# Spreading a maximum by a repeated stationary operand, one aggregate for the rest tile's statistics, and y's bound and the S sums placed earlier

## The chip, the core and the metric

One core of one Trainium2 chip. The time is device microseconds of one execution; times of several runs of a kernel are compared by their median. In the trace PE is TensorE (PEld its weight loads), DVE is VectorE, ACT is ScalarE, POOL is GpSimd and SP is SyncE, which issues most transfers.

## What is computed

Eight batches of 576 tokens go through three stages: attention by 32 memory slots per head (8 heads of 64), a channel and token mixer with width 512 and hidden width 2048, and a gated unit with a spatial product over the tokens.

```python
a = softmax(phi, axis=2)                       # over the tokens
k_m, v_m = a.T @ k, a.T @ v                    # 32 memory slots a head
x = softmax(q @ k_m.T / 8) @ v_m               # heads side by side: 576 x 512
u = x + (x.T @ U @ V).T
x = u + relu(u @ w_ch1) @ w_ch2
h = relu(x @ w_in); u, v = h[:, :512], h[:, 512:]
v = (v - mean(v)) / sqrt(var(v) + 1e-6)        # over the 512 channels
out = (u * (w_spatial @ v + b[:, None])) @ w_out
```

## The kernel before

The tokens of a batch stand in two halves of 288 columns (`TH`) or in five tiles of 128 rows, the last with 64 (the rest tile, `s == 4`). Most products run in fp16 with each operand split into a high and a low part, three matmuls for one (`HI`). Before a split the operand is scaled by a power of two found from its largest magnitude. That magnitude lies in one column, a value for each of 128 partitions, and must be known in all of them: `bmax_a` (L149) masks the exponent and scales a bf16 identity by it, which gives a diagonal; `bmax_b` (L157) multiplies the diagonal by ones, so that each partition holds all 128 values, and reduces them. GpSimd then clamps the result.

Batch 0 runs in fp32 while the weights are converted and split, with a filler that hands out that work between matmuls. Batch 1 runs the plain fp16 form (`w1_phase`, `w2_phase`, each for the halves `th` 0 and 1) and makes the sums S1 to S4 of blocks of w2 (`s_prep`, generator `sq`: load a quarter of w2, four additions, four splits, store; 11 steps a quarter, 44 in all), which batches 2 to 7 use in `st_phase`, a product with fewer multiplications. Each batch ends with its v and u tiles in the order of `V_ORDER` (`n` normalises a v tile, `y` scales the second half of y, `y_finish`), the spatial product (`spatial`) and the output product (`out_half`).

The attention of the next batch is a generator (`att`, L549). It does a step at each `yield`, and the phases call `step(nxt)` between their matmuls: in batch 1 through `w2_phase`'s `fill` (32 calls a half) and `both`, in later batches at 8 places of the first loop of `st_phase`, at each second of the first 18 of its 28 later places in the first half, and at two of three of the places of `late` in the second half, once `y_finish(b, 0)` is through; then one step behind each v or u tile. What is left is drained before the spatial phase. A "W" from it stops steps that are not asked for with `w` set.

The order on each engine is made at compile time by a scheduler that takes instructions in the order of the code where they are ready; inside `manual_schedule` (the first part of `st_phase`, and `first`) the code's order is kept as it is. PSUM holds five buffers `mm` and three buffers `at`.

In `att`, `mx` is the softmax maximum over the tokens for each memory slot, in a column a group; `dgx` holds two scaled identities, and `ones32` spreads them (L563). `scores(i)` is the i-th group of q times k_m, `ahl` the attention weights in two parts, the loop at L682 their product with U (`pps`), and `apr_sum` the result's windows. `behind_ghl` ties the reduction of phi to a place behind the spatial phase's first half.

In `v_tile` the rest tile holds its 64 rows twice, 256 channels in each half of the partitions, so that the two halves' means and variances are combined by hand (L1124 to L1136). `v_rsqrt` takes an inverse root in 13 small steps, and `v_norm` of tiles 2 to 4 waits for it.

Of the kernel before, what the change touches and what calls it, by code (L numbers as in the profile page):

```python
# [30 lines left out]
def mixer_kernel(  # L31
# [117 lines left out]
    def bmax_a(am, n=128):  # L149
        e = tiny(1, I32)  # L150
        dve.tensor_single_scalar(e[:n], am[:n].bitcast(I32), EXP_MASK, op=ALU.bitwise_and)
        dg = tp.tile([128, 128], BF16, tag="dgb", name="dgb", bufs=3)
        dve.tensor_scalar(out=dg[:n, :n], in0=identb[:n, :n], scalar1=e[:n].bitcast(F32),
                          scalar2=None, op0=ALU.mult)
        return dg

    def bmax_b(dg, o, n=128):  # L157
        ps = mm_tile()
        pe.matmul(ps[:, :n], onesb[:n, :], dg[:n, :n], start=True, stop=True)
        t = tiny()  # L160
        dve.tensor_reduce(out=t, in_=ps[:, :n], axis=AX.X, op=ALU.max)
        ps2(pool, o, t, 2.0 ** -60, ALU.max, 2.0 ** 60, ALU.min)

# [71 lines left out]
    def scale_w(name, am, n):  # L235
        dg = bmax_a(norm_bound(am, n))
# [3 lines left out]
        bmax_b(dg, C("m" + name))  # L240
# [58 lines left out]
    def first(vr):  # L299
# [7 lines left out]
        def spread(dg, n=128):  # L307
            ps = mm_tile()
            pe.matmul(ps[:, :n], onesb[:n, :], dg[:n, :n], start=True, stop=True)
            return ps  # L310

        def found(ps, o, n=128):
            t = tiny()
            dve.tensor_reduce(out=t, in_=ps[:, :n], axis=AX.X, op=ALU.max)
            ps2(pool, o, t, 2.0 ** -60, ALU.max, 2.0 ** 60, ALU.min)

# [17 lines left out]
        dgx = t1k()  # L334
        for g in range(2):
            dve.tensor_scalar(out=dgx[:, g * 128:(g + 1) * 128], in0=ident, scalar1=sc[:, g:g + 1],
                              scalar2=None, op0=ALU.mult)
        mxb = at_tile()
        pe.matmul(mxb[:, 0:256], ones32, dgx, start=True, stop=True)
# [39 lines left out]
        bu = bmax_a(norm_bound(amu, 1))  # L379
# [17 lines left out]
        bv = bmax_a(norm_bound(amv[:96], 2), 96)  # L397
# [151 lines left out]
    def att(b):  # L549
# [3 lines left out]
        dgx = t1k()  # L553
        with ExitStack() as es:
# [3 lines left out]
            for g in range(2):  # L558
                dve.tensor_scalar(out=dgx[:, g * 128:(g + 1) * 128], in0=ident, scalar1=sc[:, g:g + 1],
                                  scalar2=None, op0=ALU.mult)  # L560
# [81 lines left out]
        for gi, grp in enumerate(G):  # L642
# [28 lines left out]
            if gi == 0 and b > 2:  # L671
                scores(1)
                scores(2)
# [1074 lines left out]
```

## Time and profile before

| | us |
|---|---|
| median of 3 runs | 1134.02 (1133.17 to 1134.29) |
| profiled execution | 1134.62, span 1132.8 |

| engine | busy us | share | instructions |
|---|---|---|---|
| PE | 1112.1 | 98% | 12362 |
| PEld | 868.4 | 77% | 12365 |
| DVE | 842.9 | 74% | 2217 |
| ACT | 619.6 | 55% | 1350 |
| POOL | 89.5 | 8% | 316 |

The page's chain of work that ended last is 77% TensorE, 12% VectorE, 5% ScalarE and 2% transfers. A busy time is the union of the instructions' spans, and matmuls overlap in them: the distance from one start to the next is what a matmul costs the stream, its own duration is longer. In a timeline, neighbours of one kind are merged into one line, with the count behind an x, and a bracket gives the idle time of the engine before the line and what ended it.

### The profile page before, as it was taken

Reading aid. Unit: us, or ns where it says so; the run is one execution under the profiler, and the core shown is the slowest. Engines: PE = TensorE matmul, PEld = TensorE weight load, DVE = VectorE, ACT = ScalarE, POOL = GpSimd, SP = SyncE. Lnnn points to the kernel's source line nnn. Section 1 sums busy time; section 2 is a strip of 40 time slices with the busy share of each in tenths; the row PEclk is TensorE's granted clock in tenths of the full one; section 3 lists DMA queues with packets and bytes.
Section 4 is the critical chain, followed back from the end, with each engine's and each line's share of the span. In section 5 each row is a group of like instructions: output and inputs, shape, how many; then the busy total and the mean of one; then the engine's idle time right before and its main releaser. Section 6 shows DMA issues by size and latency. Waiting matters only on the chain.

```text
span 1132.8 us, 29695 instructions
## 1 busy us (share of the span) xinstructions
PE 1112.1 (98%) x12362; PEld 868.4 (77%) x12365; DVE 842.9 (74%) x2217; ACT 619.6 (55%) x1350; POOL 89.5 (8%) x316
## 2 busy tenths in 40 slices
PE   8899999999999999999999999999999999999998
PEld 6466767767677896788867887778967888679966
DVE  6767688878876786867776787867868687766764
ACT  4768765746546455564465454564555543653543
POOL 2101011000110001100010000100011000200000
PEclk9999999999999999999999999999999999999999
DMA  9879841351526230442316303262305303120201
GB/s 350 314 270 331 282 173 59 117 148 38 176 92 217 80 123 28 167 141 70 128 62 233 96 22 137 103 207 70 128 22 185 106 12 128 49 106 2 114 15 43
DMA packets 54855, 145.74 MB, mean 129 GB/s; under 512 B 7808, under 2 KB 37248, under 8 KB 43584
## 3 DMA queue, kind: packets, MB, share of 16 engines
q1 hardware_dynamic: 54208, 143.16, 35.9%
q8 instruction: 97, 1.59, 0.6%
q10 hardware_dynamic: 512, 0.67, 0.2%
q14 instruction: 38, 0.31, 0.1%
HBM read 120.32 MB, written 23.49 MB: 127 GB/s over the span
## 4 chain that ended last, share of the span: by engine, by line
PE 77%; DVE 12%; ACT 5%; DMA 2%; issue 2%; POOL 1%; SPq 0%; ACTq 0%; DVEq 0%; POOLq 0%
PE mm L923 17%; PE mm L957 13%; PE mm L1222 10%; PE mm L1252 8%; PE mm L1181 6%; PE mm L1110 6%; PE mm L818 4%; PE at L759 2%; PE at L578 2%; PE mm L795 1%; PE mm L841 1%; DMA gw<-in_kv_dram 1%; PE mm L878 1%; DMA wsr<-w2d 1%; DVE tmp L655 1%
## 5 line engine op out<-in xcount | busy, mean ns | idle before, releaser
L923 PE MATMUL mm<-gw,w2r 128*128 128x144 f16 x2304 | 169.6, 226 | 0.0
L923 PEld LDWEIGHTS <-w2r 128*128 128x128 f16 x2304 | 152.7, 98 | 8.7 <-issue 4.0
L957 PE MATMUL mm<-apr,z 128*128 128x288 f16 x1152 | 155.1, 286 | 0.0
L957 PEld LDWEIGHTS <-z 128*128 128x128 f16 x1152 | 109.7, 98 | 28.2 <-issue 2.0
L923 PE MATMUL mm<-gw,wa 128*128 128x144 f16 x1728 | 129.7, 226 | 0.0
L961 ACT ACTIVATE wsr<-mm 128x288 f32<-128x288 f32 x192 | 78.1, 407 | 92.5 <-PE mm L957 48.2
L1222 PE MATMUL mm<-wsr,gw 128*128 128x288 f16 x896 | 114.5, 286 | 1.7 <-ACT gw L1185 1.6
L923 PEld LDWEIGHTS <-wa 128*128 128x128 f16 x1728 | 111.1, 98 | 4.5 <-issue 1.0
L1222 PEld LDWEIGHTS <-gw 128*128 128x128 f16 x896 | 85.6, 98 | 32.2 <-issue 9.6
L1181 PE MATMUL mm<-yhl,gw 128*128 128x288 f16 x768 | 99.0, 286 | 0.0
L1252 PE MATMUL mm<-ghl,wa 128*128 128x288 f16 x768 | 97.8, 286 | 0.0
L1252 PEld LDWEIGHTS <-wa 128*128 128x128 f16 x768 | 74.4, 98 | 22.8 <-issue 3.8
L1181 PEld LDWEIGHTS <-gw 128*128 128x128 f16 x768 | 73.5, 98 | 19.0 <-issue 0.9
L1110 PE MATMUL mm<-gw,yhl 128*128 128x512 f16 x384 | 85.8, 379 | 1.3 <-ACT yhl L1076 1.3
L963 DVE TENSOR_TENSOR wsr<-wsr 128x288 f32<-128x288 f32 x96 | 44.0, 458 | 58.0 <-ACT wsr L961 58.0
L945 DVE TENSOR_TENSOR gw<-wsr,gw 128x720 f16<-128x720 f32 x96 | 85.5, 900 | 0.0
L1237 ACT ACTIVATE ghl<-gw,ysc 128x288 f16<-128x288 f32 x64 | 34.2, 535 | 83.0 <-DVE gw L1236 83.0
L944 ACT ACTIVATE gw<-wsr 128x720 f16<-128x720 f32 x96 | 76.4, 796 | 0.5
L1110 PEld LDWEIGHTS <-yhl 128*128 128x128 f16 x384 | 36.7, 98 | 43.6 <-ACT yhl L1076 1.6
L818 PE MATMUL mm<-gw,w2r 128*128 128x288 f32 x256 | 66.4, 409 | 0.1
L1116 DVE BATCH_NORM_STATS2 tiny<-tmp 128x6 f32<-128x512 f32 (+1 forms) x40 | 25.6, 639 | 46.0 <-ACT tmp L1114 46.0
L818 PEld LDWEIGHTS mm<-gw,w2r 128*128 128x128 f32 x256 | 47.4, 190 | 15.0 <-issue 1.9
(312 smaller groups left out, 1855.0 us busy)
## 6 DMA issues: line engine op xcount, KB each, us to landing
wa<-w1d SPq DMA_DIRECT2D x22, 1024.0 KB, 5.1
kvt<-in_kv_dram SPq DMA_DIRECT2D x28, 516.0 KB, 5.3
gw<-wid SPq DMA_DIRECT2D x12, 1024.0 KB, 7.8
wsr<-wsd SPq DMA_DIRECT2D x7, 1440.0 KB, 6.1
out_dram<-tmp SPq DMA_DIRECT2D x64, 144.0 KB, 1.9
gw<-in_w_dram SPq DMA_DIRECT2D x6, 1024.0 KB, 9.1
wa<-wod SPq DMA_DIRECT2D x6, 1024.0 KB, 4.8
qt<-in_qT_dram SPq DMA_DIRECT2D x23, 256.0 KB, 3.5
```

Of the source, the lines that this page charges most:

```text
L818: pe.matmul(ps, w2r[:, f, d * 128:(d + 1) * 128], AT[0]["g"][:, f, :], start=False, stop=(f == 15))
L923: pe.matmul(ps[:, dd * QH:(dd + 1) * QH], w(c, dd, 1 - x), gs[:, m, c, y, :], start=(first and c == 0 and dd == 0 and i == 0), stop=(end a ...
L944: act.activation(h, X[:, 3:8], func=ACTF.Copy)
L945: dve.tensor_tensor(out=gs[:, 2:7, c, 1, :], in0=X[:, 3:8], in1=h, op=ALU.subtract)
L957: pe.matmul(ps, a["z"][:, k, x, f * 128:(f + 1) * 128], a["apr"][:, k, y, sl], start=(i == 0), stop=(i == 5))
L961: act.activation(o, pair(ps), func=ACTF.Relu, scale=CG)
L963: dve.tensor_tensor(out=X[:, 4:6], in0=X[:, 2:4], in1=X[:, 1:3], op=ALU.subtract)
L1110: pe.matmul(ps, yhl[:, k, x, s * 128:(s + 1) * 128], wih[:, k, 0, 1 - y, :], start=(i == 0), stop=(i == 11))
L1181: pe.matmul(ps, wih[:, k, 1, 1 - x, d * 128:(d + 1) * 128], a["yhl"][:, k, y, sl], start=(i == 0), stop=(i == 11))
L1222: pe.matmul(pss[d], vn[:, s, x if s < 4 else 0, ds], wsh[:, s, th, 1 - y, :], start=(s == 0 and i == 0), stop=(s == 4 and i == 1))
L1237: act.activation(ghl[:, d, 0, sl], u2, func=ACTF.Identity, scale=sgt)
L1252: pe.matmul(ps, (wo0 if b else woh)[:, k, 1 - x, d * 128:(d + 1) * 128], a["ghl"][:, k, y, sl], start=(i == 0), stop=(i == 11))
```

## The change

- `bmax_a` and `bmax_b` go. `spread` makes the maximum itself the stationary operand, the upper 16 bits of each fp32 value repeated over 128 columns, and moves the bf16 identity through it; `found` reduces, masks the exponent and clamps; `bmax` is both. Every caller passes the column in place of the diagonal.
- The softmax maximum is spread by a transpose of its repeated column, one for each group, without `dgx`.
- In `att` from batch 3 on, `scores(2)` moves one step later; the product with U yields after slice 1 and after slice 3, in place of after slice 2, which makes one step more.
- `y_scale` is the first part of `y_finish`. For the second half it is called right behind v tile 0.
- The rest tile copies its raw statistics across the halves and aggregates once.
- In batch 1 the attention steps at three of four places of `w2_phase(b, 0)`, `sq` already steps at every second place of `w1_phase(b, 1)`, `both` has new numbers, and the rest of `sq` with the loads behind it moves from the end of `w2_phase(b, 1)` to behind v tile 0 and `y_scale`.

```diff
@@ -146,20 +146,20 @@
-    def bmax_a(am, n=128):
-        e = tiny(1, I32)
-        dve.tensor_single_scalar(e[:n], am[:n].bitcast(I32), EXP_MASK, op=ALU.bitwise_and)
-        dg = tp.tile([128, 128], BF16, tag="dgb", name="dgb", bufs=3)
-        dve.tensor_scalar(out=dg[:n, :n], in0=identb[:n, :n], scalar1=e[:n].bitcast(F32),
-                          scalar2=None, op0=ALU.mult)
-        return dg
-
-    def bmax_b(dg, o, n=128):
+    def spread(am, n=128):
         ps = mm_tile()
-        pe.matmul(ps[:, :n], onesb[:n, :], dg[:n, :n], start=True, stop=True)
+        pe.matmul(ps[:, :n], am[:n].bitcast(BF16)[:, 1:2].to_broadcast([n, 128]), identb[:n, :n],
+                  start=True, stop=True)
+        return ps
+
+    def found(ps, o, n=128):
         t = tiny()
         dve.tensor_reduce(out=t, in_=ps[:, :n], axis=AX.X, op=ALU.max)
+        dve.tensor_single_scalar(t.bitcast(I32), t.bitcast(I32), EXP_MASK, op=ALU.bitwise_and)
         ps2(pool, o, t, 2.0 ** -60, ALU.max, 2.0 ** 60, ALU.min)
+
+    def bmax(am, o):
+        found(spread(am), o)
@@ -331,12 +321,9 @@
         dve.tensor_reduce(out=sc[:, 0:2], in_=mt[:, 0:256].rearrange("p (g c) -> p g c", g=2), axis=AX.X, op=ALU.max)
-        dgx = t1k()
+        mxb = at_tile()
         for g in range(2):
-            dve.tensor_scalar(out=dgx[:, g * 128:(g + 1) * 128], in0=ident, scalar1=sc[:, g:g + 1],
-                              scalar2=None, op0=ALU.mult)
-        mxb = at_tile()
-        pe.matmul(mxb[:, 0:256], ones32, dgx, start=True, stop=True)
+            pe.transpose(mxb[:, g * 128:(g + 1) * 128], sc[:, g:g + 1].to_broadcast([128, 128]), ident)
         warm(14, mm_tile)
@@ -550,17 +537,14 @@
         mx = sc[:, 0:2]
-        dgx = t1k()
         with ExitStack() as es:
 ...
             dve.tensor_reduce(out=mx, in_=a["phiT"], axis=AX.X, op=ALU.max)
-            for g in range(2):
-                dve.tensor_scalar(out=dgx[:, g * 128:(g + 1) * 128], in0=ident, scalar1=sc[:, g:g + 1],
-                                  scalar2=None, op0=ALU.mult)
         yield
         mxb = at_tile()
-        pe.matmul(mxb[:, 0:256], ones32, dgx, start=True, stop=True)
+        for g in range(2):
+            pe.transpose(mxb[:, g * 128:(g + 1) * 128], sc[:, g:g + 1].to_broadcast([128, 128]), ident)
         e = a["e"]
@@ -670,9 +653,10 @@
                 scores(1)
+            yield
+            if gi == 0 and b > 2:
                 scores(2)
-            yield
-            if gi < 2 and b < 3:
+            elif gi < 2 and b < 3:
                 scores(gi + 1)
@@ -683,7 +667,9 @@
                           start=(s == 0 and y == 0), stop=(s == NST - 1 and y == 1))
-            if s == 2:
+            if s == 1:
+                yield
+            if s == 3:
                 yield
@@ -896,7 +881,7 @@
         dve.tensor_reduce(out=t, in_=am, axis=AX.X, op=ALU.max)
-        return y32, bmax_a(t)
+        return y32, t
@@ -1060,14 +1045,21 @@
-    def y_finish(b, th, y32, dg):
+    def y_scale(b, th, ym):
+        ysc = AT[b]["ysc"]
+        o = th * 8
+        my, ry, cs = (ysc[:, o + i:o + i + 1] for i in range(3))
+        bmax(ym, my)
+        recip(ry, my)
+        ps2(pool, cs, ry, 2.0 ** 13, ALU.mult)
+
+    def y_finish(b, th, y32, ym):
         a = AT[b]
 ...
         my, ry, cs, s_in, inv = (ysc[:, o + i:o + i + 1] for i in range(5))
-        bmax_b(dg, my)
-        recip(ry, my)
-        ps2(pool, cs, ry, 2.0 ** 13, ALU.mult)
+        if th == 0:
+            y_scale(b, th, ym)
         sl = slice(th * TH, (th + 1) * TH)
@@ -1112,28 +1104,16 @@
         act.activation(v, ps, func=ACTF.Relu, scale=inv)
-        bs = tiny(6)
-        dve.bn_stats(bs, v)
         grp, i = (0, s) if s < 2 else (1, s - 2)
 ...
         mv = a["mv", grp][:, i, :]
-        if s < 4:
-            dve.bn_aggr(mv, bs)
-        else:
-            q, m, o = tiny(2), tiny(2), mv
-            dve.bn_aggr(m, bs)
-            dve.tensor_copy(q[0:64], m[64:128])
-            dve.tensor_copy(q[64:128], m[0:64])
-            mv, t = tiny(2), tiny(2)
-            dve.tensor_scalar(out=t[:, 0:1], in0=m[:, 0:1], scalar1=q[:, 0:1], scalar2=0.5,
-                              op0=ALU.subtract, op1=ALU.mult)
-            dve.tensor_scalar(out=mv, in0=m[:, 0:2], scalar1=0.5, scalar2=None, op0=ALU.mult)
-            dve.scalar_tensor_tensor(out=mv, in0=q, scalar=0.5, in1=mv, op0=ALU.mult, op1=ALU.add)
-            dve.tensor_tensor(out=t[:, 1:2], in0=t[:, 0:1], in1=t[:, 0:1], op=ALU.mult)
-            dve.tensor_tensor(out=o[:, 1:2], in0=mv[:, 1:2], in1=t[:, 1:2], op=ALU.add)
-            dve.tensor_copy(o[:, 0:1], mv[:, 0:1])
-            mv = o
+        bs = tiny(6) if s < 4 else tiny(12)
+        dve.bn_stats(bs[:, 0:6], v)
+        if s == 4:
+            dve.tensor_copy(bs[0:64, 6:12], bs[64:128, 0:6])
+            dve.tensor_copy(bs[64:128, 6:12], bs[0:64, 0:6])
+        dve.bn_aggr(mv, bs)
         nm = tiny()
@@ -1586,16 +1566,27 @@
                 nb[0] += 1
-                if nb[0] < 8 or nb[0] % 3 == 0:
-                    step(nxt, nb[0] > 8)
+                if nb[0] < 12 or nb[0] % 2 == 0:
+                    step(nxt, nb[0] > 12)
                 next(sq, None)
-            y0 = w2_phase(b, 0, lambda: step(nxt), lambda f: fl.until(s2, min(f + 3, 16)))
-            w1_phase(b, 1, nofill, y_finish(b, 0, *y0))
+            n0 = [0]
+
+            def most():
+                n0[0] += 1
+                if n0[0] % 4:
+                    step(nxt)
+
+            y0 = w2_phase(b, 0, most, lambda f: fl.until(s2, min(f + 3, 16)))
+            n1 = [0]
+
+            def ahead():
+                n1[0] += 1
+                if n1[0] % 2 == 0:
+                    next(sq, None)
+
+            w1_phase(b, 1, ahead, y_finish(b, 0, *y0))
             y1 = w2_phase(b, 1, both)
-            drain(sq)
-            load_s4()
-            load_ws()
         else:
@@ -1620,7 +1611,12 @@
         vt = {0: v_tile(b, 0)}
+        y_scale(b, 1, y1[1])
         vf = (lambda: vfill(0.1)) if b == 0 else (lambda: step(nxt, True))
+        if b == 1:
+            drain(sq)
+            load_s4()
+            load_ws()
         if b == 0:
```

## Rows read from the trace of the kernel before

**Rows 1.** Stages: length, busy us of each engine (xinstructions), granted clock, DMA share, GB/s.

```profile
214.00:309.00 95.00, 92.56 (x899) 68.91 (x897) 79.10 (x210) 54.29 (x123) 6.15 (x23) 1.00 0.36 112
352.60:484.30 131.70, 131.28 (x1649) 106.00 (x1647) 99.83 (x264) 69.03 (x154) 9.50 (x35) 1.00 0.33 114
```

**Rows 2.** Timeline, repeating batch: start us, us, engine, line, operation, tiles, shapes.

```profile
388.62 0.32 PE L622 MATMUL at<-gw,t1k 64*32 64x64 f32 x8 [0.21 <-ACT tmp L627]
426.37 0.27 PE L684 MATMUL at<-ahl,u3h 128*128 128x256 f16 x1 [0.21 <-DVE ahl L670]
```

**Rows 3.** Timeline of TensorE, batch 1.

```profile
240.65 0.67 PE L622 MATMUL at<-qt,t1k 64*32 64x128 f32 x32
...
245.63 0.67 PE L622 MATMUL at<-qt,t1k 64*32 64x128 f32 x32 [0.71 <-DMA qt<-in_qT_dram]
...
252.31 0.91 PE L878 MATMUL mm<-gw,w2r 128*128 128x288 f16 x6 [0.21 <-DVE w2r L171]
...
302.64 0.22 PE L159 MATMUL mm<-dgb,onesb 128*128 128x128 bf16 x1
...
308.61 5.47 PE L1110 MATMUL mm<-gw,yhl 128*128 128x512 f16 x24 [1.34 <-ACT yhl L1076]
```

**Rows 4.** Timeline, end of the v phase: batch 0 (first row), last batch.

```profile
186.10 4.08 PE L1222 MATMUL mm<-wsr,gw 128*128 128x288 f16 x32 [1.07 <-ACT gw L1185]
...
1098.24 0.18 DVE L1125 BATCH_NORM_AGGREGATE tiny<-tiny 128x2 f32<-128x6 f32 x1
...
1099.55 0.17 DVE L1149 TENSOR_SCALAR ve<-mv 128x3 f32<-128x3 f32 x1
...
1102.02 1.33 ACT L1163 ACTIVATE gw<-tmp,mv 128x512 f16<-128x512 f32 x2 [1.13 <-DVE mv L1158]
...
1104.95 4.20 PE L1222 MATMUL mm<-wsr,gw 128*128 128x288 f16 x33 [0.53 <-ACT gw L1185]
```

**Rows 5.** Timeline of TensorE, batch 0.

```profile
90.68 0.22 PE L159 MATMUL mm<-dgb,onesb 128*128 128x128 bf16 x1 [0.23 <-DVE dgb L153]
```

**Rows 6.** Groups by line, whole span: busy us, mean ns | idle before, releaser.

```profile
L153 DVE TENSOR_SCALAR dgb<-identb,tiny 128x128 bf16<-128x128 bf16 (+1 forms) x53 | 13.4, 253 | 1.4
...
L159 PE MATMUL mm<-dgb,onesb 128*128 128x128 bf16 x51 | 11.2, 220 | 0.3 <-DVE dgb L153 0.2
...
L151 DVE TENSOR_SCALAR tiny<-tiny 128x1 int32<-128x1 int32 (+1 forms) x53 | 7.8, 147 | 1.2
...
L159 PEld LDWEIGHTS <-onesb 128*128 128x128 bf16 x51 | 5.0, 98 | 2.9 <-issue 1.0
```

**Rows 7.** Chain of work that ended last, first 60 us: start us, us, what.

```profile
2.45 11.16 DMA gw<-in_kv_dram
```

**Rows 8.** Timeline of TensorE: the pair of transposes, and the spread by ones.

```profile
346.15 0.59 PE L563 MATMUL at<-t1k,ones 128*128 128x256 f32 x2
346.58 0.65 PE L1252 MATMUL mm<-ghl,wa 128*128 128x288 f16 x4
...
381.74 0.38 PE L598 MATMUL at<-ident,nkv 128*128 128x128 f32 x2
381.96 0.91 PE L923 MATMUL mm<-gw,w2r 128*128 128x144 f16 x12
```

**Rows 9.** Timeline of VectorE and ScalarE, batch 1.

```profile
300.32 0.45 DVE L165 TENSOR_REDUCE tiny<-mm 128x1 f32<-128x288 f32 x1
...
306.49 0.28 DVE L161 TENSOR_REDUCE tiny<-mm 128x1 f32<-128x128 f32 x1
...
308.02 1.81 ACT L1076 ACTIVATE yhl<-y,ysc 128x288 f16<-128x288 f32 x4
```

**Rows 10.** Timeline of SyncE's queue, end of batch 0.

```profile
198.60 0.32 SPq L1038 DMA_DIRECT2D wsr<-w2d  x1
```

**Rows 11.** Timeline of ScalarE, end of a repeating batch's v phase.

```profile
451.69 1.51 ACT L724 ACTIVATE apr<-at,sc 128x384 f16<-128x384 f32 x3
453.08 0.52 ACT L743 ACTIVATE vmu<-t1k,rq 128x256 f16<-128x256 f32 x1
```

More of the change, by code (lines that the diff above doesn't have):

```diff
@@ L235, in scale_w @@
     def scale_w(name, am, n):
-        dg = bmax_a(norm_bound(am, n))
+        nb = norm_bound(am, n)
         yield 0.6
@@ L239, in scale_w @@
         yield 0.6
-        bmax_b(dg, C("m" + name))
+        bmax(nb, C("m" + name))
         yield 0.6
@@ L305, in first @@
         stack.enter_context(tc.manual_schedule())
[L307 to L315, printed above, removed]
         warm(36, mm_tile)
@@ L378, in first @@
                           in1=rd.unsqueeze(2).to_broadcast([128, 2, 128]), op=ALU.mult)
-        bu = bmax_a(norm_bound(amu, 1))
+        bu = norm_bound(amu, 1)
         warm(7, mm_tile)
@@ L396, in first @@
         found(pu, C("mU"))
-        bv = bmax_a(norm_bound(amv[:96], 2), 96)
+        bv = norm_bound(amv[:96], 2)
         recip(C("rU"), C("mU"))
@@ L609, in att @@
         absmax(av, vmt32)
-        dg = bmax_a(av)
         G = ((0, 1), (2, 3), (4,))
@@ L632, in att @@
         mv, rv, sv = sc[:, 4:5], sc[:, 5:6], sc[:, 6:7]
-        bmax_b(dg, mv)
+        bmax(av, mv)
         recip(rv, mv)
@@ L713, in att @@
         dve.tensor_reduce(out=am[:, 3:4], in_=am[:, 0:3], axis=AX.X, op=ALU.max)
-        dg = bmax_a(am[:, 3:4])
         yield
@@ L718, in att @@
         mA, rA, sA, cA = (sc[:, 7 + i:8 + i] for i in range(4))
-        bmax_b(dg, mA)
+        bmax(am[:, 3:4], mA)
         recip(rA, mA)
@@ L898, in w2_phase @@
         dve.tensor_reduce(out=t, in_=am, axis=AX.X, op=ALU.max)
-        return y32, bmax_a(t)
+        return y32, t
     QH = TH // 2
@@ L1026, in st_phase @@
         dve.tensor_reduce(out=t, in_=am, axis=AX.X, op=ALU.max)
-        return Y, bmax_a(t)
+        return Y, t
     def s_prep():
@@ L1190, in u_half @@
                 dve.tensor_reduce(out=t, in_=us, axis=AX.X, op=ALU.max)
-                a["dg", th] = bmax_a(t)
+                a["um", th] = t
     def g_scale(b, th):
@@ L1197, in g_scale @@
         mg, sgt, isg = (a["ysc"][:, o + i:o + i + 1] for i in (5, 6, 7))
-        bmax_b(a["dg", th], mg)
+        bmax(a["um", th], mg)
         pmul(mg, mg, C("K"))
```

## The prediction, made before the changed kernel ran

> **What bounds the kernel now.** Read the busy time of each engine by stage first. Two stages tell it: one batch of the repeating part (352.6 to 484.3 us, and four more like it) has TensorE busy 131.28 of 131.70 us, batch 1 (214 to 309 us) 92.56 of 95.00, both at the full granted clock [rows 1]. So the change can pay in two ways only: it makes TensorE's own stream shorter, or it closes one of the few holes in that stream. Work taken from VectorE alone is worth nothing unless a hole hangs on it. After the stages, read TensorE's timeline for its holes, each with what ended it: two of 0.21 us in the repeating batch [rows 2], 0.71, 0.21 and 1.34 us in batch 1 [rows 3], 1.07 us at the end of batch 0's statistics and 0.53 us at the same place in the last batch [rows 4], 0.23 us in batch 0 [rows 5].
>
> **Spreading a maximum (53 places).** Before, VectorE masks the exponent (L151, 147 ns) and scales an identity to a diagonal (L153, 253 ns); TensorE multiplies it by ones (L159, 128 columns of bf16 with a 98 ns weight load); VectorE reduces [rows 6]. After, the maximum itself is the stationary operand, repeated over 128 columns, and the identity moves; the mask follows the reduction. The multiply has the same 128 columns, so TensorE's stream is unchanged by this, 0. VectorE loses 53 x 0.253 = 13.4 us of busy time, beside TensorE nearly everywhere, so 0 on the path. Latency: 0.147 + 0.253 = 0.40 us less ahead of the multiply and 0.147 more behind it. One thing is new: the weight load cannot start before the value is there, where ones could be loaded early. Its cost lies between 0 (value ready while earlier matmuls run) and 0.098 us in each of the 53 (5.2 us); I take 0 for nearly all, since only one of the 51 multiplies of L159 has idle put down to its diagonal [rows 5, 6]. That one, 0.23 us at 90.68 us in batch 0, is the place where the shorter lead pays: 0.40 earlier less 0.10 for the load closes it, and I take 0.2. In the first 60 us the same saving lies on VectorE, while the chain there begins with an 11.16 us load of k and v [rows 7] and the extra mask comes later on the same engine: 0, within 0.2 either way.
>
> **The softmax maximum of each batch (7 places).** The two scalings of an identity and one fp32 multiply by ones (two records, 256 columns each) give way to two transposes of a repeated column. The multiply takes TensorE from 346.15 to 346.58 us, 0.43 us until the next matmul; a pair of fp32 transposes of the same 128x128 shape takes from 381.74 to 381.96, 0.22 us [rows 8]. The gain is 0.21 x 7 = 1.5 us, in a stream that has no holes there. The bound below it: if the new pair holds the engine for its whole 0.38 us [rows 8], 0.05 x 7 = 0.35 us.
>
> A page speaks against this item. The Trainium skill, in "TensorE: Matmul & The Clock Gate", section "Part 4: PE-mode transpose", measures about 275 ns for one transpose in a kernel. Taken as time that the engine is held, two would be 0.55 us against 0.43 and the item a loss of 0.8 us (an estimate from that page). The pair here disagrees: both are through in 0.22 us, and the page's figure is a latency.
>
> **Scores and the product with u, one step later (5 batches, 2 to 6).** The copies of the first scores out of PSUM end a 0.21 us hole, because two score groups follow each other on three buffers; the second group moves to the next step, which is already in the second half's product phase. This hole goes whole: 5 x 0.21 = 1.1 us. The other 0.21 us is the third slice's product, waiting for the low half of the attention weights; its step comes one call of six 144-column matmuls later. It ends between 0.21 (hidden) and 0 (the last slice, also one step later, waits instead); I take 0.15, x 5 = 0.7 us. Together 1.8. The added step also pushes everything behind it in that generator (the apr sums, their scale, the vmu products) one slot later in the v phase; the cover there is the u matmuls. What if it fails is the third rival.
>
> **Batch 1.** Three moves. Score steps are spread to three of four slots, so that the second scores come five slots after the first in place of four: today they start 4.98 us apart, 0.71 of it waiting for the load of q; a slot is six 288-column matmuls, 0.91 us with the last one's latency and somewhat less without [rows 3], so 0 to 0.1 is left, gain 0.6. The 0.21 us wait for the split of w2 sits in the same crowd on VectorE; gain 0.2 at most, I take 0.15. Then y's bound: VectorE reads the last maximum only at 300.32 us, because the last group's sums and splits are queued ahead of it; the reduction of the spread bound follows at 306.49, ScalarE's first scaled y at 308.02, and TensorE waits 1.34 us [rows 3, 9]. The change puts the spread one v tile sooner (two of them are the 5.47 us of the last row of [rows 3], so 2.7 us) and holds the last splits back behind it. What is late next is ScalarE: it now gets the four held splits before y, and TensorE may wait at the spread itself. So between 0 and 1.34, and I take 0.9. The loads of the S4 blocks and of w_spatial, which move behind this point too, cost 0: SyncE's queue holds nothing urgent behind them, and their readers are the spatial phase and the next batch; if that cover went, a whole load would be open. On GpSimd the bound's two small steps now pass the second v tile's negated mean, 0 as well. Together 1.65.
>
> **Statistics of the rest tile (8 batches).** From its aggregate at 1098.24 to the first step of the root at 1099.55 are 1.31 us in nine dependent steps; two copies and one aggregate remain, about 0.6 (three starts some 0.2 apart, as the first of the nine). With the diagonals gone from between the root's steps, some 0.8 us less. It pays where ScalarE's norm, which waits for the root (1.13 us idle at 1102.02), releases the buffer that TensorE wants [rows 4]: 0.53 in the last batch (all of it) and 0.85 of 1.07 in batch 0. The wider statistics take one of the four wide small buffers that the attention's softmax uses; no softmax runs in this phase, so 0. In the other six batches the first z product stands there and no hole exists: 0. Together 1.4.
>
> **The sum.** 1.5 + 1.8 + 1.65 + 1.4 + 0.2 = 6.55 us. The profiled execution took 1134.62 us, 0.60 above the median of 1134.02; 1134.62 - 6.55 = 1128.1, and against the median 1127.5.
>
> **The rivals.** First, *the moves do little*: position in the code is only a wish, since the compiler's scheduler orders each engine; the load of w2 for batch 1's sums was issued at 198.60 us, in batch 0, while the code asks for it only in batch 1's second w2 phase [rows 10]. Then batch 1 and the repeating batches keep their holes in other places and only 1.5 + 1.4 + 0.2 = 3.1 remain: 1130.9. For it: that row. Against it: the two holes of the repeating batch lie in stretches where the code's order was visibly kept.
>
> Second, *batch 1 backfires*: the spread now stands ahead of v tile 1 in TensorE's queue, and 2.7 us before the 302.64 at which it stood, at 299.9. If the last maximum is still read at 300.32 us, it is there at 300.32 + 0.45 and some 0.2 for the reduction after it, 301.0, and TensorE waits 1.1 us in place of the gain of 1.65: 6.55 - 1.65 - 1.1 = 3.8 left, 1130.2.
>
> Third, and slower: *the later step collides*. In the batches 2 to 6 ScalarE scales apr (1.51 us) and vmu (0.52) just before the norms of the v tiles [rows 11]. If the added step lets them fall between the norms of tiles 2 and 4, the spatial matmuls wait for the last tile by up to 2.03 us in each of five batches, 10.2 us against a gain of 6.55: 1137.6. It decides from a delay of 1.3 us a batch. For it: no slack shows between those norms and the matmuls. Against it: ScalarE sat idle just before the norms in the last batch [rows 4], the root ends sooner, and the norms have their place in the code ahead of most of the moved work.
>
> Fourth, *a transpose holds TensorE for its whole length*, the bound above: 1.5 becomes 0.35, 1128.6. The page's figure is the stronger form of this.
>
> **How the numbers follow.** Forecast 0.55, 1127.5; moves do little 0.22, 1130.9; batch 1 backfires 0.09, 1130.2; collision 0.10, 1137.6; transposes 0.04, 1128.6. A measurement of this kernel can tell 0.2%, 2.3 us, from no change, so faster means below 1131.7. The forecast and the transposes lie there whole, two thirds of the first rival (0.15) and half of the second (0.05): 0.79. The rest of these is no change, 0.11, the collision is slower, 0.10. Range: at the low end every hole named here is gone and the first 60 us give their 0.2, 1.5 + 2.1 + 2.3 + 1.6 + 0.4 = 7.9 us, 1126.1, less half a us for interplay, 1125.6; at the high end 1132.5 takes in the first two rivals with 1.6 us for what they may cost besides. It leaves out the collision and about as much again.
>
> **What would show it.** L159's place shows no diagonals, VectorE some 20 us less busy. The holes behind the copies of scores and at the third slice of the product are gone in each of five batches, the transposes leave 0.22 us, not 0.38, to the next matmul. In batch 1 ScalarE's first scaled y of the second half comes before TensorE has done the third u block. In batch 0 and the last batch the spatial matmuls wait under 0.25 us. It would be wrong if the same holes return one step later, if a spread shows a wait of the weight load in many places, or if the norms of tiles 2 to 4 stand behind apr's scaling in the repeating batches.

## The result and the profile after

The changed kernel took 1124.87 us (median of 6 runs, 1122.57 to 1126.19) against 1134.15 us before (6 runs, 1133.17 to 1134.75): ratio 0.9915, 95% interval 0.9902 to 0.9928. The gain is 9.3 us where 6.6 were forecast; the forecast of 1127.5 us had the direction right and the size too small, and the measured time lies 0.7 us below its low end of 1125.6. The profiled execution has a span of 1123.6 us, 9.2 less than before.

Span, and busy time of each engine; below it the shares of the chain that ended last:

```profile
span 1123.6 us, 29563 instructions
...
PE 1106.3 (98%) x12362; PEld 868.0 (77%) x12365; DVE 823.1 (73%) x2100; ACT 619.4 (55%) x1350; POOL 88.2 (8%) x316
...
PE 84%; DVE 7%; ACT 4%; DMA 3%; issue 1%; POOL 0%; SPq 0%; DVEq 0%; POOLq 0%; ACTq 0%
```

VectorE is 19.8 us less busy than before, as forecast. TensorE is 5.8 us less busy with the same number of matmuls, where the forecast had 1.5 from the transposes, and its share of the chain that ended last rose from 77% to 84%, VectorE's fell from 12% to 7%: waits for VectorE went.

To see where the time went, the span of each profiled execution is cut at the same four points of TensorE's stream: the first product of batch 0's first layer, and the first output product of batches 0, 1 and 6. In us:

| stage | before | after | gain | forecast |
|---|---|---|---|---|
| up to batch 0's first layer | 38.72 | 38.26 | 0.46 | 0 |
| batch 0 | 160.10 | 160.23 | -0.13 | 1.26 |
| batch 1 | 140.56 | 140.12 | 0.44 | 1.86 |
| the five batches 2 to 6 | 658.85 | 650.73 | 8.12 | 2.85 |
| batch 7 and the end | 134.59 | 134.23 | 0.36 | 0.53 |

(The forecast is cut to these stages with the transposes' 0.21 us where they stand, one in batch 0, one in batch 1 and five in the five batches; so cut, its terms add up to 6.50.) So the repeating batches gave 5.3 us more than forecast, and batches 0 and 1 together 2.8 less. The stage rows of after that answer to [rows 1]: batch 1, one repeating batch, and the five together; then the five of the kernel before:

```profile
198.49:338.61 140.12, 137.92 (x1385) 100.35 (x1383) 113.84 (x297) 80.67 (x182) 13.01 (x41) 1.00 0.34 115
468.76:598.91 130.15, 130.15 (x1649) 105.72 (x1647) 97.30 (x251) 69.02 (x154) 8.70 (x35) 1.00 0.34 115
338.61:989.34 650.73, 650.73 (x8233) 528.58 (x8230) 485.26 (x1250) 345.34 (x771) 43.43 (x174) 1.00 0.33 111
```

```profile
339.39:998.24 658.85, 656.55 (x8232) 529.69 (x8230) 498.44 (x1320) 345.64 (x771) 47.00 (x174) 1.00 0.32 110
```

Here is the puzzle of the case. In the five batches TensorE showed 658.85 - 656.55 = 2.30 us of idle time before and none after, and yet 8.12 us went. The other 5.8 came out of time that the profile calls busy. The transposes account for 5 x 0.21 = 1.1 of it.

**Where busy time hid a stall.** The product with u, before, four lines around the hole of [rows 2] (start, length, line, tiles, count):

```profile
425.66 0.49 PE L684 MATMUL at<-ahl,u3h 128*128 128x256 f16 x3
...
426.48 1.29 PE L923 MATMUL mm<-gw,w2r 128*128 128x144 f16 x18
427.60 0.76 PE L684 MATMUL at<-ahl,u3h 128*128 128x256 f16 x4
428.19 0.29 PE L923 MATMUL mm<-gw,w2r 128*128 128x144 f16 x2
```

and after:

```profile
424.06 0.60 PE L668 MATMUL at<-ahl,u3h 128*128 128x256 f16 x4
424.50 0.54 PE L908 MATMUL mm<-gw,w2r 128*128 128x144 f16 x6
424.87 0.60 PE L668 MATMUL at<-ahl,u3h 128*128 128x256 f16 x4
425.31 1.29 PE L908 MATMUL mm<-gw,w2r 128*128 128x144 f16 x18
```

Read the distance from the first start to the start behind the group, not the lengths. Four undisturbed products of one slice take 424.50 - 424.06 = 0.44 us, 0.11 each. Before, the slice from 425.66 took 426.48 - 425.66 = 0.82, a loss of 0.38, of which [rows 2] shows 0.21 as idle. The slice from 427.60 took 0.59, a loss of 0.15 with no idle shown at all. One such matmul is recorded with 0.27 us [rows 2] and followed after 0.11 by the next when nothing holds it; so the first 0.16 us of a stall behind such a product lie under its recorded tail.

The scores' hole of [rows 2] reads the same way. Its line of four matmuls before, and the same matmuls undisturbed after:

```profile
387.99 0.42 PE L923 MATMUL mm<-gw,wa 128*128 128x144 f16 x4
```

```profile
386.85 1.30 PE L908 MATMUL mm<-gw,wa 128*128 128x144 f16 x18
387.99 1.73 PE L908 MATMUL mm<-gw,w2r 128*128 128x144 f16 x25
```

Undisturbed, 18 of them take 387.99 - 386.85 = 1.14 us, four 0.25. Before, four took 388.62 - 387.99 = 0.63: 0.38 lost, 0.21 of it shown.

The same holds at a place that I had taken to have no stall, the first z product of the next batch at the end of the v phase. Before (TensorE, then VectorE), and after:

```profile
717.75 1.18 PE L759 MATMUL at<-wa,vmt 64*32 64x512 f16 x24
718.86 0.42 PE L1222 MATMUL mm<-wsr,gw 128*128 128x288 f16 x2
...
717.43 0.61 DVE L725 SCALAR_TENSOR_TENSOR apr<-at,sc,apr 128x384 f16<-128x384 f32 x1
```

```profile
712.74 0.84 PE L744 MATMUL at<-wa,vmt 64*32 64x512 f16 x24
713.51 0.66 PE L1202 MATMUL mm<-wsr,gw 128*128 128x288 f16 x4
...
711.36 0.61 DVE L710 SCALAR_TENSOR_TENSOR apr<-at,sc,apr 128x384 f16<-128x384 f32 x1
```

1.11 us from start to start before, 0.77 after: 0.34 us, again with no idle shown. The trace releases the second of these products by the second apr sum on VectorE, which ended at 718.04, 0.29 behind the chunk's start; after, it ends at 711.97, 0.77 ahead of it. Each of these products is recorded with 0.37 to 0.39 us, so the whole wait lies under the record of the first one: how much a stall can hide is the recorded length of the matmul ahead of it, less the distance at which the next one would follow.

Summed by line over one repeating batch (602.78 to 734.51 us before, 598.91 to 729.05 after), the distances between starts on TensorE fell by 0.54 us in the product with u, 0.40 at the scores and the matmuls ahead of them, 0.34 in the z products, 0.21 at the transposes and 0.10 in the spatial products: 1.59 together, the whole of 131.73 - 130.14.

### The profile page after: what moved, and what is told of

It reads as the page before. It is cut to its first block, busy times and chain, and to the rows that moved or that the text cites. A ratio compares the mean times of both kernels' runs of the same rounds, so it can differ in the third digit from the quotient of the medians.

```text
span 1123.6 us, 29563 instructions
## 1 busy us (share of the span) xinstructions
PE 1106.3 (98%) x12362; PEld 868.0 (77%) x12365; DVE 823.1 (73%) x2100; ACT 619.4 (55%) x1350; POOL 88.2 (8%) x316
## 4 chain that ended last, share of the span: by engine, by line
PE 84%; DVE 7%; ACT 4%; DMA 3%; issue 1%; POOL 0%; SPq 0%; DVEq 0%; POOLq 0%; ACTq 0%
PE mm L908 23%; PE mm L942 13%; PE mm L1202 10%; PE mm L1232 8%; PE mm L1161 6%; PE mm L1102 6%; PE mm L803 4%; PE mm L826 2%; PE at L562 2%; PE at L744 2%; PE mm L863 2%; PE mm L780 1%; PE mm L919 1%; DMA gw<-in_kv_dram 1%; PE at L605 1%
## 5 line engine op out<-in xcount | busy, mean ns | idle before, releaser
L863 PE MATMUL mm<-gw,w2r 128*128 128x288 f16 x384 | 50.6, 286 | 0.4 <-DVE w2r L171 0.4
```

The costliest lines, as they stand in the source:

```text
L863: pe.matmul(pss[d], w2h[:, f, 1 - x, d * 128:(d + 1) * 128], g[:, f, y, :], start=False, stop=(f == 15 and i == 2))
```

## The experiments

Twelve kernels: each part of the change alone on the kernel before, parts taken out of the changed kernel, and variants of batch 1. Timed runs of one kernel differ by 0.1 to 0.5%, more than most parts are worth, so the verdicts rest on the length of the stages above, each in one profiled execution; the times stand beside them. "A repeating batch" is a typical one of the five. All in us:

| run | batch 0 | batch 1 | five batches | a repeating batch | median, ratio to before (95%) |
|---|---|---|---|---|---|
| before | 160.10 | 140.56 | 658.85 | 131.73 | |
| changed | 160.23 | 140.12 | 650.73 | 130.15 | 1124.87, 0.9902 to 0.9928 |
| e1 moves alone | 160.16 | 141.43 | 654.09 | 130.73 | 1129.89, 0.9938 to 0.9968 |
| e2 statistics alone | 159.72 | 141.73 | 657.94 | 131.53 | 1131.92, 0.9960 to 0.9987 |
| e3 transposes alone | 160.03 | 140.91 | 657.63 | 131.47 | 1133.88, 0.9983 to 1.0006 |
| e4 spreads alone | 160.02 | 140.87 | 659.84 | 131.76 | 1135.93, 1.0000 to 1.0022 |
| e5 batch 1's parts alone | 160.13 | 140.50 | 658.70 | 131.76 | 1135.28, 1.0000 to 1.0023 |
| e6 changed, bound late | 158.65 | 143.48 | 650.89 | 130.15 | 1126.58, 0.9920 to 0.9950 |
| e7 changed, sums not ahead | 158.57 | 139.30 | 650.76 | 130.15 | 1124.16, 0.9893 to 0.9926 |
| e8 changed, spreads behind | 158.85 | 139.90 | 650.97 | 130.15 | 1124.12, 0.9899 to 0.9928 |
| e9 changed, no moves | 160.63 | 140.11 | 655.97 | 131.20 | 1129.01, 0.9940 to 0.9964 |
| e10 changed, old statistics | 159.20 | 141.10 | 652.51 | 130.36 | 1128.48, 0.9924 to 0.9967 |
| e11 changed, diagonals | 159.74 | 139.77 | 652.04 | 130.29 | 1126.09, 0.9903 to 0.9946 |
| e12 changed, plain steps | 159.16 | 139.58 | 650.69 | 130.14 | 1123.95, 0.9887 to 0.9933 |

The two theories that matter: *S*, the idle that the profile shows is the price of a stall, on which the forecast rests; *H*, the price is the distance between starts, and the profile hides the first 0.16 us of each.

In three runs, one of the five batches is longer than the others because TensorE waits once for a load of w1, which none of their edits touches; in the five batches of the other eleven profiles no such wait shows. In e4 and e11:

```profile
995.56 0.84 PE L747 MATMUL at<-wa,vmt 64*32 64x512 f16 x24 [0.64 <-DMA wa<-w1d]
```

```profile
473.04 0.84 PE L756 MATMUL at<-wa,vmt 64*32 64x512 f16 x24 [0.51 <-DMA wa<-w1d]
```

In e10 it is 0.60. From start to start e4 loses 0.71 us by it, e10 0.67 and e11 0.58. So in these runs the typical batch says what the edit is worth, and the sum of the five does not.

**e1, the moves alone.**

```diff
@@ kernel before
                 scores(1)
-                scores(2)
             yield
+            if gi == 0 and b > 2:
+                scores(2)
-            if gi < 2 and b < 3:
+            elif gi < 2 and b < 3:
...
-            if s == 2:
+            if s == 1:
+                yield
+            if s == 3:
                 yield
```

> The kernel before with one part of the change: the second score group and the last slice of the product move one step later; everything else is as before. Theory S (the shown idle is the price, as forecast): 5 batches x (0.21 + 0.15) = 1.8 us faster, a repeating batch 0.36 us shorter. Theory H (a stall costs the whole distance between two starts on TensorE, and the profile shows as idle only what goes beyond some 0.16 us of each): the product's two stalls are 0.374 and 0.164 us, the scores' 0.378 and a little, so 5 x (0.54 + 0.40) = 4.7 us faster, a repeating batch 0.94 us shorter. Theory V (the long gain of the repeating batch comes from VectorE's lighter load and not from the moves): under 1.8 us.

A repeating batch became 1.00 us shorter, five batches 4.76. S's number (0.36, 1.8) and V's fall. H's (0.94, 4.7) holds, in part by luck: by lines it is 0.40 at the scores, as H said, 0.41 in the product, where H had 0.54, and 0.20 in the z products that no theory had named for this run.

**e9, the same from the other side**: the changed kernel with these lines as before.

> The changed kernel with the second score group and the last slice of the product back at their old steps; all else as changed. Theory S (idle is the price): 1.8 us slower, a repeating batch 0.36 us longer. Theory H (start to start): the stalls of 0.54 us in the product and 0.40 us at the scores return, a repeating batch 0.94 us longer, 4.7 us in all. Theory I (the parts lean on one another: with the spreads alone the wait at the scores was 0.29 us longer, which shows only when the moves are not there): 1.2 us per batch, 6 us in all.

Five batches 5.24 us longer, 1.05 each, between H and I. The stage, and the hole that answers to the first of [rows 2]:

```profile
339.07:995.04 655.97, 653.23 (x8232) 529.33 (x8230) 484.68 (x1250) 345.81 (x771) 43.48 (x174) 1.00 0.33 110
```

```profile
388.37 0.32 PE L605 MATMUL at<-gw,t1k 64*32 64x64 f32 x8 [0.50 <-ACT tmp L610]
```

655.97 - 653.23 = 2.74 us of idle came back and cost 5.24. The wait at the scores is now 0.50 where it was 0.21 before, the same 0.50 as with the spreads alone (e4 below).

**e2, the rest tile's statistics alone** (the aggregate and the steps behind it replaced by two copies and one aggregate, as in the diff of the change), **and e10, the changed kernel with the nine steps.**

> The kernel before with the rest tile's statistics aggregated in one step, nothing else. Theory S: 1.4 us faster (0.85 in batch 0, 0.53 in the last batch), a repeating batch unchanged. Theory H: besides, VectorE comes to the apr sums sooner in every v phase, the last of them releases the PSUM tile that the first z product waits for (0.34 us between two starts, none of it shown as idle), and the spatial stage loses 0.10 us of stall: a repeating batch 0.3 to 0.45 us shorter, 3 to 3.5 us faster in all. Theory D (the diagonals do that, not the statistics): 1.4 us and a repeating batch within 0.1 us of before.

> The changed kernel with the rest tile's statistics in nine steps as before. Forecast: 1.4 us slower, in batch 0 and in the last batch, a repeating batch unchanged. Theory H1 (the first z product's wait for the last apr sum returns whole): a repeating batch 0.34 us longer besides, 3.1 us in all. Theory H2 (the other parts have brought the sums forward enough; alone they took 0.20, 0.09 and 0.07 of the 0.34): a repeating batch up to 0.1 us longer, 1.4 to 1.9 us in all.

Alone they close the z product's stall whole:

```profile
718.86 0.84 PE L759 MATMUL at<-wa,vmt 64*32 64x512 f16 x24
719.63 1.61 PE L1210 MATMUL mm<-wsr,gw 128*128 128x288 f16 x10
```

0.77 from start to start, so D falls and H's mechanism holds; but the spatial products then wait 0.11 longer, and a batch gained 0.20, less than H said. In batch 0 the wait of 1.07 [rows 4] shrank to 0.58 by this part alone, and the last batch's went.

Taken out of the changed kernel they cost 0.21 in a repeating batch, 0.12 at the z products and 0.10 in the spatial ones: between H2 and H1, nearer to H2. No theory named batch 1, which is 0.98 us longer than in the changed kernel, 0.69 of it at this wait and most of the rest at the spread of y's bound:

```profile
324.35 4.20 PE L1214 MATMUL mm<-wsr,gw 128*128 128x288 f16 x33 [0.95 <-ACT gw L1177]
```

The changed kernel waits 0.26 there. In batch 0 and the last batch the same wait is 0.76 and 0.94, against 0.14 and 0.15. So outside the five batches this part is worth about 2 us in the company of the others.

**e3, the transposes alone.**

> The kernel before with the softmax maxima by two transposes each, nothing else. As forecast: 0.21 us shorter per batch, 1.5 us in all. If a transpose held TensorE for its length: 0.05 per batch, 0.35 in all. If VectorE's two scalings less (0.85 us per batch) closed a stall besides: more than 0.25 us per batch.

0.26 per repeating batch, 0.21 of it at the transposes, as forecast, and the rest at the z products: there VectorE's lighter load took a little from a stall, as the third theory has it. By the times alone none of this could be told, their interval reaches from 1.9 us faster to 0.7 slower.

**e4, the spreads alone, and e11, the changed kernel with the diagonals back.**

> The kernel before with only the maxima spread by a repeated stationary column in place of diagonals; y's bound stays where it was. As forecast: 0.2 us faster, a repeating batch within 0.05 us of before. Theory D (the diagonals' absence brings the apr sums forward and closes the z product's stall): a repeating batch 0.3 us shorter, 1.7 us faster in all. Theory W (a weight load that must wait costs at some spreads, and TensorE's order in batch 0 lets one spread wait 1.7 us for the norm of w2): 1 to 2 us slower.

> The changed kernel with the diagonals back: each maximum masked, scaled into a diagonal and multiplied by ones; all else as changed. Forecast: 0.2 us slower, nothing in a repeating batch. Theory I (the spreads pay in the repeating batches once the moves have taken the scores' wait away; the four parts alone sum to 6.0 of 8.1 us there): 0.2 to 0.4 us per repeating batch, 1 to 2 us slower.

Alone, a repeating batch is as long as before (131.76) for three reasons that cancel: the product loses one stall (0.18) and the z products 0.09, the scores' wait grows by 0.29:

```profile
387.75 0.32 PE L611 MATMUL at<-gw,t1k 64*32 64x64 f32 x8 [0.50 <-ACT tmp L616]
```

In the changed kernel, where the moves have taken that wait away, they are worth 0.14 us in a repeating batch (130.29 against 130.15), 0.11 of it in the product, about 0.7 in five. The 1.31 us by which the five batches are longer without them would fit theory I, but 0.58 of it is the wait for the load shown above: I has the sign and is too large. D falls (0.09 of its 0.3 at the z products), and so does W's place: in e4 the spread in question waits 0.22 us, and batch 0 is no longer than before. The time alone, 0.9 us slower with an interval of 0 to 2.5, would have allowed W's 1 to 2.

**e5, batch 1's parts alone** (the steps of scores and sums, y's bound one v tile sooner, diagonals kept).

> The kernel before with the two parts of batch 1 alone: the score steps and sums spread differently, and y's bound one v tile sooner with the last splits behind it; the diagonals stay. Forecast: 1.65 us faster (the wait for q 0.6, the split of w2 0.15, y's bound 0.9). Theory K (what the chip showed of the whole change: three stalls of 0.5, 0.2 and 0.2 us in batch 1's second first-layer phase, since the sums' splits now run on ScalarE and VectorE beside it, and a spread that waits about 0.65 us for the last maximum): the gain is 0 to 0.5 us.

Batch 1 is 140.50 against 140.56: theory K's size. But this stage is not steady: e1 to e4, which leave these two parts out, have 140.87 to 141.73, and the spread of y's bound waits 0.46 to 1.08 us in three of them where it waits 0.04 in the profile of before. Against the mean of before and these four, 141.1, the parts gave 0.6.

**e6, the changed kernel with y's bound late** (the early call taken out, the bound computed where y is scaled).

> The changed kernel with y's bound put back to where it stood before (the spread after the second v tile), the last splits of the sums still behind the first v tile. Forecast: the hole of 1.34 us before the last rest tile's products returns: 0.9 us slower. Theory K: the 1.34 us return and the 0.65 us at the early spread go: 0.7 us slower. Theory N (the late splits alone do it): no difference.

Batch 1 became 3.4 us longer than in the changed kernel, more than any theory said:

```profile
307.62 1.81 ACT L1067 ACTIVATE yhl<-y,ysc 128x288 f16<-128x288 f32 x4 [0.74 <-POOL ysc L142]
...
308.21 1.16 PE L1101 MATMUL mm<-gw,yhl 128*128 128x512 f16 x4 [2.64 <-ACT yhl L1067]
```

The held splits of the sums now run on ScalarE and VectorE ahead of y: its first scaling starts 11.9 us behind the first v product (295.76), against 9.0 in the changed kernel and 10.8 before. (In e1 and e2, whose steps up to there are those of before, it is 11.8, so the step from 10.8 to 11.9 says little.) At 143.48 this batch is also longer than the 140.56 to 141.73 of the runs without either edit: here the splits behind the first v tile, without the bound ahead of them, did not pay.

**e7, the changed kernel without the sums' steps in the second first-layer phase.**

```diff
-            w1_phase(b, 1, ahead, y_finish(b, 0, *y0))
+            w1_phase(b, 1, nofill, y_finish(b, 0, *y0))
```

> The changed kernel, with no steps of the sums in batch 1's second first-layer phase, as before; the rest of the batch 1 schedule as changed, so that the eight steps are done later, behind y's bound. Theory K: the stalls of 0.49, 0.16 and 0.21 us in that phase go, 0.8 to 0.9 us faster, if nothing is late next. Rival: the eight steps now lie behind the spread and hold up ScalarE's scaled y or the norms: the stall comes back in the v phase, 0 to 1.5 us slower.

Batch 1 is 0.82 us shorter, the number of theory K, and not by K's mechanism. The three stalls are still there; what is gone is the wait of 0.65 us at the spread, with 0.81 between starts there:

```profile
261.12 2.37 PE L826 MATMUL mm<-apr,z 128*128 128x288 f16 x18 [0.49 <-ACT tmp L830]
268.84 3.10 PE L826 MATMUL mm<-apr,z 128*128 128x288 f16 x24 [0.15 <-ACT gw L832]
272.38 0.86 PE L856 MATMUL mm<-apr,vmu 32*64 32x288 f16 x22 [0.21 <-ACT gw L832]
...
301.95 0.22 PE L151 MATMUL mm<-identb,tiny 128*128 128x128 bf16 x1
```

So theory K is wrong about what holds that phase. That the edit took the wait at the spread away is not shown: e12, which has the same edit and one more, waits 0.53 us there.

**e12, besides, one score step to every slot of the first second-layer phase, as before.**

```diff
-                if n0[0] % 4:
-                    step(nxt)
+                step(nxt)
```

> The changed kernel with batch 1's score steps one to a slot in its first second-layer phase, and no steps of the sums in the second first-layer phase, both as before; y's bound early and the last splits behind it, as changed. Theory M (the spacing of the score steps carries the softmax of the last group into the change of phase, where ScalarE's copies hold TensorE): the stalls of 0.41, 0.49, 0.15 and 0.21 us shrink to the 0.21 of before, the wait for q of 0.7 us returns: batch 1 0.1 to 0.4 us shorter than without the sums' steps alone (139.30 us from one output phase to the next). Rival: the four stalls stay, and the wait for q comes on top: 0.7 us longer.

```profile
243.52 0.67 PE L605 MATMUL at<-qt,t1k 64*32 64x128 f32 x32 [0.49 <-DMA qt<-in_qT_dram]
248.43 0.91 PE L863 MATMUL mm<-gw,w2r 128*128 128x288 f16 x6 [0.15 <-DVE w2r L171]
254.92 3.11 PE L863 MATMUL mm<-gw,w2r 128*128 128x288 f16 x24 [0.17 <-DVE w2r L171]
...
298.90 0.23 PE L151 MATMUL mm<-identb,tiny 128*128 128x128 bf16 x1 [0.53 <-DVE tiny L883]
```

The stalls at the change of phase are gone and the wait for q is back, as theory M says of the mechanism. Yet batch 1 is 139.58 against 139.30 without this edit, not shorter: between starts, 1.04 us less at the change of phase, 0.8 more in the attention's products and those of w2, 0.14 less in the spatial products, and 0.70 more in the v tiles, where the spread waits again. Without that last term it would be 0.42 shorter, about M's number; whether the edit brings that wait or the execution does is not shown.

**e8, the changed kernel with two spreads further back in TensorE's queue** (for that, the last steps of w_out's norm are called later in the code).

```diff
-        bmax(nb, C("m" + name))
+        with tc.issue_after(last[0].ins) if name == "o" else ExitStack():
+            ps = spread(nb)
+        found(ps, C("m" + name))
...
+                if hook and i == 6:
+                    with tc.issue_after(m.ins):
+                        hook()
```

> The changed kernel with two spreads put further back in TensorE's queue: that of the norm of w_out in batch 0 behind the third block of the second first-layer phase, and that of y's bound in batch 1 behind the sixth matmul of v tile 1 (the last splits of the sums go behind it there). Theory W (a spread at the head of TensorE's queue costs what its maximum is late): 1.72 + 0.65 = 2.4 us faster. Rival: the time is lost to the next late thing (the chain behind the maximum is as late as before, 0 to 0.5 us faster).

Both waits at the spreads are gone, and the next late things are these:

```profile
102.13 1.09 PE L566 MATMUL at<-kvt,e 128*32 128x129 f32 x32 [0.96 <-ACT e L556]
...
321.74 0.53 PE L1209 MATMUL mm<-wsr,gw 128*128 128x288 f16 x3 [0.87 <-ACT gw L1172]
```

The rival holds: batch 1 gained 0.22, and batch 0 is no shorter than in e6 and e7 without the edit. For batch 0 that is a weak test: ScalarE shows no wait for w_out's load in any of these three, and the spread waited only 0.35 and 0.23 us in e6 and e7. None of e7, e8 and e12 can be told from the changed kernel by its time (the intervals lie over one another).

## Why the prediction was right in direction and short in size

**What bounds the kernel** was read rightly: the stream of TensorE and its holes. The step that failed is the reading of a hole's size. The prediction measured the transposes from start to start, and the holes by their idle time. The idle time of [rows 2] is the price less 0.16 us, and stalls that fit under the record of the matmul before them do not show. The terms that this left short, in the five batches: 1.8 us forecast for the scores and the product, 4.7 measured; nothing for the z products, 1.7 measured; nothing for the spatial products, 0.5 measured. e1, e2 and e9 show the first two by single edits.

The Trainium skill says in "Perfetto Trace Analysis", section "Identifying the Most-Contended Engine", that the busy share of matmuls is not a good measure of how close a kernel is to the roofline, because pipelined instructions look smaller in the trace, and names the busy share of weight loads, beside another figure, to use in its place. The trace agrees with the rule, for another reason: in the five batches before, matmuls were busy 656.55 of 658.85 us, 99.7%, since their records hid the stalls, and 8.12 us, 1.2%, could still be had; weight loads were busy 529.69 us, 80%.

**The softmax maximum**: right, with its number. The transposes leave 0.22 us to the next matmul:

```profile
345.37 0.38 PE L547 MATMUL at<-ident,sc 128*128 128x128 f32 x2
345.59 1.14 PE L1232 MATMUL mm<-ghl,wa 128*128 128x288 f16 x8
```

against the 0.43 of [rows 8]. Rival four, that a transpose holds the engine for its whole length, falls, in its stronger form too.

**Scores and product**: right mechanism, mis-sized terms. Forecast 1.1 + 0.7 us; measured 5 x 0.40 = 2.0 and 5 x 0.54 = 2.7 (the latter 0.41 a batch by the moves, the rest by the spreads and their lighter VectorE). The first rival, that the moves do little, falls with e1 and e9. The third, slower one did not come: ScalarE still scales apr ahead of the norms of tiles 2 to 4, as it did in [rows 11], and no wait shows at the spatial products of the five batches. (The sign that the prediction named for this rival, norms behind apr's scaling, held before the change already, 454.68 behind 451.69 us, and could not tell.)

```profile
449.13 1.52 ACT L709 ACTIVATE apr<-at,sc 128x384 f16<-128x384 f32 x3 [0.53 <-POOL sc L142]
...
452.36 1.33 ACT L1143 ACTIVATE gw<-tmp,mv 128x512 f16<-128x512 f32 x2 [0.34 <-DVE mv L1138]
```

**Statistics of the rest tile**: the chain is as forecast:

```profile
1089.73 0.17 DVE L1114 COPY tinyw<-tinyw 64x6 f32<-64x6 f32 x1
...
1090.35 0.17 DVE L1129 TENSOR_SCALAR ve<-mv 128x3 f32<-128x3 f32 x1
...
1095.67 1.51 PE L1202 MATMUL mm<-wsr,gw 128*128 128x288 f16 x11 [0.15 <-ACT gw L1165]
```

0.62 us from the first copy to the root (0.6 forecast), and the wait of 0.53 in the last batch [rows 4] is 0.15. In batch 0 the 1.07 of [rows 4] went too; 0.14 is left, and by e2 this part alone leaves 0.58. "In the other six batches the first z product stands there and no hole exists: 0" was the wrong sentence: 0.34 us stood there under the tail of a matmul, 1.7 us in five batches, and e2 shows that this part alone closes it.

**Spreading a maximum**: nothing of the stream changed, and the weight load of a repeated column takes 99 ns where ones took 98 [rows 6]:

```profile
L151 PE MATMUL mm<-identb,tiny 128*128 128x128 bf16 (+1 forms) x53 | 11.6, 220 | 2.7 <-DVE tiny L232 1.7 <-DVE tiny L883 0.6 <-DVE tiny L165 0.3
...
L151 PEld LDWEIGHTS <-tiny 128*128 128x128 bf16 (+1 forms) x53 | 5.2, 99 | 5.8 <-DVE tiny L232 2.5 <-DVE tiny L883 1.1 <-DVE tiny L165 0.5
```

Three of 53 spreads wait, 2.7 us in all, against 0.3 before. The largest, 1.72 us in batch 0, ate what that batch had gained:

```profile
98.82 0.23 PE L151 MATMUL mm<-identb,tiny 128*128 128x128 bf16 x1 [1.72 <-DVE tiny L232]
...
91.10 1.19 ACT L198 ACTIVATE wa<-wsr 128x1024 f32<-128x1024 f32 x1 [1.43 <-DMA wsr<-in_w_out_dram]
```

Its maximum is late because ScalarE waited 1.43 us for a load of w_out; in e6, where that load was there, the same spread waits 0.35 us and batch 0 is 158.65 long, 1.45 less than before. So the forecast of 1.26 for batch 0 fits executions in which the load is early, and the profiled one is not among them; the other changed kernels go the same way: in e12 ScalarE waits 0.51 us for that load, the spread 0.81, and batch 0 is 159.16 long; in e9 1.60, 1.92 and 160.63; in e7 no wait for the load, 0.23 and 158.57. That the moved place in TensorE's queue (after 24 of 32 matmuls of w2, after 30 before) is what exposes it was argued from the order of the rows; e8, which moved it back, does not settle it, since in its profile the load was early.

**Batch 1**: the two big holes of [rows 3] went, and others came. The scores start at 242.75 and 247.68 us without a wait. ScalarE's first scaled y comes at 306.18, 9.0 us behind the first v product in place of 10.8 and ahead of the end of the third u block near 307.6, as the prediction said it would, and the rest tile's products wait no more. But:

```profile
253.15 0.91 PE L863 MATMUL mm<-gw,w2r 128*128 128x288 f16 x6 [0.40 <-DVE w2r L171]
...
258.94 2.37 PE L826 MATMUL mm<-apr,z 128*128 128x288 f16 x18 [0.48 <-ACT tmp L830]
...
300.59 0.23 PE L151 MATMUL mm<-identb,tiny 128*128 128x128 bf16 x1 [0.65 <-DVE tiny L883]
...
324.18 2.00 PE L1202 MATMUL mm<-wsr,gw 128*128 128x288 f16 x15 [0.26 <-ACT gw L1165]
```

With 0.16 and 0.21 us more in the same phase these are 2.16 of shown idle, 1.95 more than the 0.21 that the first of these places had in [rows 3], against 0.71 + 1.34 gone. The second rival had the place (the spread waits for the last maximum), with a price of 1.1 where 0.65 is shown and 0.81 lost; what the forecast missed is that score steps set later carry the last softmax into the change of phase (e12).

The sum: 5.3 us more in the repeating batches, 1.4 less in batch 1, 1.4 less in batch 0, 0.2 less in the last batch, 0.5 more before them: 2.7 us, the difference between 9.3 and 6.6. That the whole missed by no more than this is luck: two misses of opposite sign, 5.3 and 2.8, stood against each other.

## What to carry to other kernels

Price a stall on TensorE by the distance between two starts, against the same pair where nothing waits, and not by the idle time shown; a batch in which TensorE looks busy throughout can still give over 1%. Look for the release of every matmul that starts later than its neighbours' step, also where no idle stands ahead of it. And where a stage's queue is full, moving a step trades one wait for another: take the next late thing into the sum before the gain. A batch that repeats says most: take its typical length, and look at the one that differs for a wait that the edit does not explain.

## What the runs showed that was not expected

- A wait of up to 0.16 us behind one of the products with u shows no idle at all, and a longer one shows that much less: 0.21 shown, 0.38 lost. Behind the first of the z products, recorded with 0.39 us, 0.34 us were lost and none shown.
- The parts lean on one another less than their sums suggest. In the five batches the four parts that bear on them gave 4.76, 0.91, 1.22 and -0.99 us alone, 5.9 together, and the whole gave 8.12; but 0.71 of the -0.99 is the wait for a load of w1, and the first of e1's five batches gained 0.5 us less than the others. In a typical batch the parts alone gave 1.00, 0.20, 0.26 and -0.03, together 1.43, and the whole 1.58. Taken out of the changed kernel, the moves cost 1.05, the statistics 0.21 and the spreads 0.14: only the spreads gain by company, by 0.17 us a batch.
- Before batch 0's first layer the executions here took 37.3 to 42.1 us; the longest has TensorE waiting 1.6 us for a load of q. Differences of whole times under some 2 us say little about one edit. The typical length of a batch that repeats does, within some 0.05 us; batch 0 and batch 1, which each profile has once, moved by 1 us and more with waits that no edit explains.
